# Attention and routed experts on one Trainium2 core: one load per head for both row tiles of a pair, and smaller pieces of the first experts' weights

## The chip, the cores and the metric

The kernel runs on one core of a Trainium2 chip. The metric is the device time of one execution in microseconds (us), lower is better. Engines are called TensorE (PE, with its weight loads as PEld), VectorE (DVE), ScalarE (ACT), GpSimd (POOL) and SyncE (SP), which only issues transfers here.

## What is computed

Two parts follow one another. First, local attention over chunks of 64 positions; then a mixture of eight experts in which each token goes to one expert and each expert keeps at most `capacity` tokens (80).

```python
q_c, k_c, v_c = (a.reshape(B, H, nc, 64, D) for a in (q, k, v))   # B=8, H=8, S=576, D=64
scores = q_c @ k_c.transpose(0, 1, 2, 4, 3) / 8
attn = exp(scores - scores.max(-1)); attn /= attn.sum(-1) + 1e-9
x = (attn @ v_c) as (B*S, H*D) = (4608, 512)

logits = x @ w_gate                       # 8 experts
e = argmax(logits); gate = softmax(logits)[e]
for e in range(8):                        # at most 80 tokens each, those of the largest gate
    out[tok] = gate[tok] * (relu(x[tok] @ w1[e]) @ w2[e])   # 512x1024 and 1024x512, f32
```

Rows of `out` whose token was not kept are zero.

## The kernel before

**Attention.** The 4608 rows are 36 row tiles of 128, taken as 18 pairs (`NPAIR`). A tile's queries and keys are 128 rows of 1024 f32 in memory (`qk`). They go into a tile of three parts of 512 columns (`qb`), the rows of one head half at columns 0 to 1023 and those of the other at 512 to 1535, each on every second partition; the corners stay zero from memsets at the start, so that one matmul does two heads. Each tile therefore has two loads of 64 rows of 4 KB (`load_qk`, L320 to L325), 256 KB each. The values have two loads of 64 rows of 2080 bytes per tile (`load_v`, L330 to L332), 130 KB each. Six buffers of each kind hold three pairs.

The loop over pairs (L688 to L734) is software-pipelined. Step n runs the scores of pair n (L341, 32 matmuls), the transposes of finished rows of pair n-3 (`px`, L366), the values of pair n-2 (L394), the transposes of probabilities of pair n-1 (`pt`, L366), on VectorE the maxima and differences of pair n and the division of pair n-2, and then the store of pair n-2 to scratch (`xs`, L422, 512 KB). Every second step has the gate's matmuls for four tiles (L446) and the steps of the gating chain. The transfers of a step are all issued by SP, in the order in which the program writes them: after `scores(n)` the first tile of pair n+3, then the values of the first tile of pair n+1, the second tile of pair n+3, the values of the second tile, then the store. An instruction that waits on SP holds up everything behind it. `order` below is that program order.

**Opening** (L635 to L672). VectorE and GpSimd clear the buffers; TensorE runs 25 matmuls on a cleared tile (`warm`); SP issues queries and keys of pairs 0, 1 and 2, values of pairs 0 and 1, the constants (`ct`, `wgp`, `capi`), and the values of pair 2. Pair 3 is issued in step 0, after all of these.

**Weights of the first two experts.** `EARLY` names the steps at which pieces of experts 0 and 1 are issued (`early_weights`, L622 to L633): eight pieces of 1 MB, pieces 0 to 5 at steps 15 to 19 (18 and 19 stand for the two places behind the loop), pieces 6 and 7 behind it. The last two are held back by a small copy on GpSimd into the target (L630) that reads a column of `bo`, a result of the gating chain.

**Selection** (L736 to L888). The end of the gating chain finds each expert's threshold, ranks the tokens kept and makes the lists of rows. `hot` (L585) makes the one-hot matrices: five of them by VectorE into tiles `pk` that take over the memory of five `qb` buffers. `keep_warm` (L607) runs matmuls whose result nobody reads. GpSimd then gathers the kept rows from `xs`, six indirect transfers of 128 rows (`gather`, L175); the first one ends TensorE's wait.

**Experts** (L171 to L278). Six row tiles go through both layers (`hc` L202, `yc` L235). The third expert's first weights are issued by `part(2, 0)` (L916) ahead of the gathers; the rest, and the stores of zeros to `out`, follow by the list `LATER`, each `part` of list 0 only after a gathered tile has landed (L905). Of the names in the listings, `w1_2` is the first layer's weights of expert 2.

Of the kernel before, what the change touches and what calls it, by code (L numbers as in the profile page):

```python
# [21 lines left out]
NB = 3  # L22
NBV = 6
NT = 9
# [16 lines left out]

EARLY = {15: [0], 16: [1], 17: [2, 3], 18: [4], 19: [5]}

# [12 lines left out]
def attention_moe(ctx: ExitStack, tc: tile.TileContext, qk, vv, wg, w1, w2, cap, cst, out):  # L56
# [225 lines left out]
    with ExitStack() as actx:  # L282
# [14 lines left out]
        TT = {}  # L297
        QKV = {}
        XT = {}
# [13 lines left out]
        def flush(queue):  # L313
            while queue:
                step_one(queue)

        qbufs = [wk.tile([P, 3 * 512], F32, name=f"qb{j}", tag=f"qb{j}", bufs=1)
                 for j in range(2 * NB)]

        def load_qk(i, eng=nc.sync):  # L320

            d = QKV["qk", i] = qbufs[i % (2 * NB)]
            for h in range(2):
                eng.dma_start(d[h:P:2, 512 * h:512 * h + 1024],  # L324
                              qk[i // 2, i % 2, 64 * h:64 * h + 64])  # L325

        vbufs = [wk.tile([P, 2, VW], F32, name=f"vb{j}", tag=f"vb{j}", bufs=1)
                 for j in range(NBV)]

        def load_v(i):  # L330
            for h in range(2):
                nc.sync.dma_start(vbufs[i % NBV][h:P:2, h], vv[i // 2, i % 2, h])  # L332

        def scores(n):
            d = U[n] = {}
            ps = d['s'] = ps1.tile([P, 2, 512], F32, name=f"s{n}", tag="o" if n == 1 else "s")
            for t in range(2):
                t8 = QKV["qk", 2 * n + t].rearrange("p (w a u s) -> p w a u s", w=3, a=4, u=2)
                for pr in range(4):
                    for u in range(2):  # L340
                        nc.tensor.matmul(  # L341
                            ps[64 * u:64 * u + 64, t, P * pr:P * pr + P].rearrange(
                                "p (h k) -> p h k", h=2),
                            lhsT=t8[:, 1, pr, u, :], rhs=t8[:, 0:3:2, pr, u, :],
                            start=True, stop=True)
# [31 lines left out]
        def values(i, tag=None):  # L377
# [3 lines left out]
            if r == 0:  # L381
                TT[T] = wk.tile([P, 4, DM], F32, name=f"x{T}", tag="x")
            v = vbufs[i % NBV].rearrange("p h (a u x) -> p h a u x", a=4, u=2)
            if tag is None:
# [200 lines left out]
        def hot(rt, way, n):  # L585

            if way == "v":
                j = S['hot'] = S.get('hot', -1) + 1
                oh = wk.tile([P, P, HOT], BF16, name=f"pk{rt}", tag=f"qb{j}", bufs=1)
                nc.vector.tensor_tensor(  # L590
# [31 lines left out]
        def early_weights(n, after=None):  # L622

            e, c = divmod(n, 4)
            if c == 0:
                weights[e] = tiles_w(wp, e)
            j = c % 2
            w, src, m = ((weights[e][0], w1, 2), (weights[e][1], w2, 4))[c // 2]
            if after is not None:
# [5 lines left out]
        with tc.manual_schedule():  # L635
            warm = gk.tile([P, 2 * P], BF16, name="warm", tag="lv", bufs=LV)
            nc.vector.memset(warm, 0.0)
            for j, qb in enumerate(qbufs):
                eng = nc.gpsimd if j == 1 else nc.vector
                eng.memset(qb[:, 0:512], 0.0)  # L640
                eng.memset(qb[:, 1024:1536], 0.0)  # L641
                if j < 2:
                    load_qk(j, (nc.sync, nc.scalar)[j])
            nc.scalar.dma_start(ident, cst[:, C_ID:C_ID + P])
            for j, vb in enumerate(vbufs):
                (nc.vector if j in (0, 2) else nc.gpsimd).memset(vb, 0.0)
            nc.vector.memset(wgp[:, :, 8:32], 0.0)
# [11 lines left out]
            nc.scalar.mul(idp, ident, float(P))  # L659
            for i in (2, 3):  # L660
                load_qk(i)
            for i in (0, 1):
                load_v(i)
            for i in (4, 5):
                load_qk(i)
            for i in (2, 3):
                load_v(i)
            nc.sync.dma_start(ct[:, C_ID + P:], cst[:, C_ID + P:])
            nc.sync.dma_start(wgp[:, :, 0:8], wg.rearrange("(b p) e -> p b e", p=P))
            nc.sync.dma_start(capi, cap[0:1, :].broadcast_to([P, 2]))  # L670
            for i in range(4, NBV):
                load_v(i)  # L672

# [14 lines left out]
            for n in range(NPAIR):  # L688
                odd = n % 2
                if n == 2:  # L690
                    late_constants()
                scores(n)
                if n + NB < NPAIR:
                    load_qk(2 * (n + NB))
                    if n < 2:
                        load_qk(2 * (n + NB) + 1)
                if n >= 5 and odd:
# [3 lines left out]
                if n >= 2:  # L701
                    for t in range(2):
                        values(2 * (n - 2) + t)
                        if n - 2 + NBV // 2 < NPAIR:
                            load_v(2 * (n - 2) + t + NBV)
                        if t == 0 and n + NB < NPAIR:
                            load_qk(2 * (n + NB) + 1)
                if n >= 1:
# [71 lines left out]
            for j in range(33, 36):  # L780
                steps_(nc.vector, j)
            for k in (6, 7):
                early_weights(k, bo[:, 28 + 4 * (k - 6):29 + 4 * (k - 6)])
            tally(28, 4)
# [88 lines left out]

            keep_warm(6)

# [194 lines left out]
```

## Time and profile before

| | us |
|---|---|
| three timed runs | 259.73, 262.20, 262.93 (median 262.20) |
| the profiled execution | 259.46 |
| its span, first to last instruction | 257.7 |

The span is what the profile shows; the remaining 1.8 us of the profiled execution lie outside it. All times in the rows are us from the start of the span. A row with "x" and a number merges that many instructions; what stands in brackets or behind "<-" is what ended the idle time before it. The granted clock (PEclk) is TensorE's clock as a share of 2.4 GHz; 0.5 is 1.2 GHz.

### The profile page before, as it was taken

The page shows a single profiled execution, that of the slowest core. Times are in us where ns is not written, and L with a number is a line of the kernel's source. Part 1 is how long each engine was busy: PE and PEld are TensorE (multiplying, and loading weights), DVE is VectorE, ACT ScalarE, POOL GpSimd, SP SyncE. Part 2 cuts the span into 40 slices and gives each one's busy share as a digit, 9 for nine tenths or more (in the row PEclk, how much of TensorE's full clock was granted, in tenths as well). Part 3 has the DMA queues.
Part 4 walks back from the last instruction along what each step waited for, and adds up shares of the span by engine and source line. Part 5 has one row for each costly group of instructions (what it writes and reads, how often), then busy time and mean ns, then how long its engine had stood idle before and what let it go on. Part 6 is the DMA issues. An engine that isn't in the chain of part 4 may idle for free.

```text
span 257.7 us, 7341 instructions
## 1 busy us (share of the span) xinstructions
PE 227.0 (88%) x3117; PEld 145.5 (56%) x3117; DVE 118.7 (46%) x263; ACT 66.2 (26%) x115; POOL 56.9 (22%) x167
## 2 busy tenths in 40 slices
PE   6851999999999988798878858999999999999990
PEld 4751988898889877687756742343433434333320
DVE  7924376967869675677658360111111102112200
ACT  1202133535537352536354001120100202001000
POOL 9003000023332222213848354000000000000261
PEclk9998599999999999999997795999999999999996
DMA  5868999999999989999999998999999999999240
GB/s 206 282 217 243 365 346 327 308 326 320 304 311 334 315 293 317 310 318 295 332 405 413 410 392 281 401 393 411 416 409 401 416 408 413 410 397 404 111 156 36
DMA packets 35766, 84.73 MB, mean 329 GB/s; under 512 B 4048, under 2 KB 4176, under 8 KB 35728
## 3 DMA queue, kind: packets, MB, share of 16 engines
q1 hardware_dynamic: 34464, 80.73, 86.8%
q0 software_dynamic: 960, 2.88, 3.1%
q10 hardware_dynamic: 304, 0.59, 0.7%
q8 instruction: 27, 0.44, 0.7%
q14 instruction: 11, 0.09, 0.1%
HBM read 64.00 MB, written 20.45 MB: 328 GB/s over the span
## 4 chain that ended last, share of the span: by engine, by line
PE 68%; DMA 10%; SPq 9%; DVE 4%; POOL 3%; issue 3%; ACT 0%; POOLq 0%; DVEq 0%
PE hc L202 17%; PE yc L235 16%; PE o L394 10%; PE s L341 9%; DMA qb<-in_qk 5%; SPq L332 5%; PE px L366 4%; SPq L324 3%; PE small L446 3%; PE pt L366 3%; DMA vb<-in_vv 3%; DMA xgc<-xs,gic 2%; PE hpc L220 2%; PE xpc L190 1%; DVE qb L641 1%
## 5 line engine op out<-in xcount | busy, mean ns | idle before, releaser
L341 PE MATMUL s<-qb 128*64 128x128 f32 x576 | 38.1, 284 | 13.1 <-DMA qb<-in_qk 12.9
L202 PE MATMUL hc<-w,xtc 128*32 128x512 f32 x384 | 45.5, 619 | 0.0
L235 PE MATMUL yc<-w,htc 128*32 128x512 f32 x384 | 42.3, 592 | 0.0
L341 PEld LDWEIGHTS s<-qb 128*64 128x64 f32 x576 | 32.7, 141 | 16.8 <-issue 10.7
L394 PE MATMUL o<-vb,pT 128*64 128x130 f32 x576 | 36.4, 278 | 1.0 <-DMA vb<-in_vv 1.0
L351 DVE TENSOR_REDUCE mx<-s 128x16 f32<-128x1024 f32 x18 | 22.0, 1224 | 25.7 <-PE s L341 25.7
L394 PEld LDWEIGHTS o<-vb,pT 128*64 128x64 f32 x576 | 31.9, 136 | 2.2 <-PE px L366 1.1
L235 PEld LDWEIGHTS yc<-w,htc 128*32 128x32 f32 x384 | 12.4, 110 | 28.3 <-issue 28.3
L202 PEld LDWEIGHTS hc<-w,xtc 128*32 128x32 f32 x384 | 12.1, 114 | 27.8 <-issue 27.4
L375 ACT ACTIVATE pT<-pt 128x1024 f32<-128x1024 f32 x18 | 18.4, 1024 | 28.9 <-PE pt L366 28.9
L437 ACT COPY xT<-px 128x1024 f32<-128x1024 f32 x17 | 17.2, 1011 | 33.5 <-PE px L366 33.5
L254 POOL DMA_INDIRECT out<-ysc,to x6 | 6.0, 994 | 88.4 <-SPq L921 84.7
L409 DVE TENSOR_TENSOR x<-o,rc 128x1024 f32<-128x1024 f32 (+1 forms) x20 | 22.4, 1118 | 0.7
L356 DVE TENSOR_TENSOR sm<-s,mx 128x1024 f32<-128x1024 f32 x18 | 22.1, 1229 | 0.6
L207 ACT ACTIVATE hsc<-hc 128x512 f32<-128x512 f32 x6 | 3.6, 598 | 65.3 <-PE hc L202 65.3
L240 DVE TENSOR_SCALAR ysc<-yc,gatec 128x512 f32<-128x512 f32 x6 | 4.5, 752 | 33.4 <-PE yc L235 33.4
L209 DVE TENSOR_SCALAR hsc<-hc 128x512 f32<-128x512 f32 x6 | 4.2, 692 | 26.6 <-PE hc L202 26.6
L224 DVE COPY htc<-hpc 128x512 f32<-128x512 f32 x6 | 4.2, 692 | 22.0 <-PE hpc L220 22.0
L366 PE MATMUL pt<-ct,sm 64*128 64x64 f32 x288 | 12.8, 229 | 1.6 <-ACT pT L375 1.2
L366 PE MATMUL px<-ct,x 64*128 64x64 f32 x288 | 13.2, 234 | 0.0
L511 POOL TENSOR_SCALAR u<-sx 128x4 f32<-128x4 f32 x8 | 1.6, 195 | 52.4 <-DVE sx L510 40.8
L366 PEld LDWEIGHTS pt<-ct,sm 64*128 64x128 f32 x288 | 10.4, 139 | 4.8 <-issue 2.8
(133 smaller groups left out, 226.3 us busy)
## 6 DMA issues: line engine op xcount, KB each, us to landing
w<-in_w SPq DMA_DIRECT2D x12, 2048.0 KB, 17.6
qb<-in_qk SPq DMA_DIRECT2D x70, 256.0 KB, 4.8
vb<-in_vv SPq DMA_DIRECT2D x72, 130.0 KB, 4.3
out<-zero SPq DMA_DIRECT2D x9, 1024.0 KB, 16.9
xs<-x SPq DMA_DIRECT2D x16, 512.0 KB, 4.6
w<-in_w SPq DMA_DIRECT2D x8, 1024.0 KB, 11.7
xs<-x SPq DMA_DIRECT2D x4, 256.0 KB, 10.5
qb<-in_qk ACTq DMA_DIRECT2D x2, 256.0 KB, 3.6
```

The lines of the kernel that those rows point to most:

```text
L202: nc.tensor.matmul(h[o:o + 32, :], lhsT=xT[r][:, b, o:o + 32], rhs=getw(groups[r][g])[0][:, b, 512 * f:512 * f + 512], start=(b == 0), sto ...
L235: nc.tensor.matmul(y[o:o + 32, :], lhsT=hT[r][c // 4][:, c % 4, o:o + 32], rhs=getw(groups[r][g])[1][:, c, :], start=(c == 0), stop=(c == ...
L324: eng.dma_start(d[h:P:2, 512 * h:512 * h + 1024], qk[i // 2, i % 2, 64 * h:64 * h + 64])
L332: nc.sync.dma_start(vbufs[i % NBV][h:P:2, h], vv[i // 2, i % 2, h])
L341: nc.tensor.matmul(ps[64 * u:64 * u + 64, t, P * pr:P * pr + P].rearrange("p (h k) -> p h k", h=2), lhsT=t8[:, 1, pr, u, :], rhs=t8[:, 0:3 ...
L351: nc.vector.tensor_reduce(d['mx'], d['s8'], axis=AX.X, op=ALU.max)
L356: nc.vector.tensor_tensor(d['sm'].rearrange("p c k h -> p h c k"), d['s8'], d['mx'][:, :, :, None].to_broadcast([P, 2, 8, 64]), op=ALU.sub ...
L366: nc.tensor.transpose(pm[:, u, 64 * c:64 * c + 64], src(c)[rows], ident[rows, rows])
L375: nc.scalar.activation(d['pT'], pt, AF.Exp, scale=0.125)
L394: nc.tensor.matmul(po[64 * u:64 * u + 64, o:o + 130].rearrange("p (h x) -> p h x", h=2), lhsT=d['pT'][:, u, c:c + 64], rhs=v[:, :, pr, u, ...
L409: nc.vector.tensor_tensor(TT[T][:, r:r + nt, :].rearrange("p r (k h e) -> p (r k) h e", k=4, h=2), pov[..., 0:64], rc[:, :, :, None].to_br ...
L437: nc.scalar.copy(dst, pm)
```

## The change

- `load_qk(n)` and `load_v(n)` load one head half of both row tiles of a pair with one transfer: 64 rows, two pieces of 4 KB each (512 KB), and two pieces of 2080 bytes (260 KB). A pair has 5 transfers instead of 9. The buffers are three tiles of double size. `load_qk(n + 3)` is issued after all of the scores of pair n, `load_v(n + 1)` after both tiles' values of pair n-2.
- In the opening the two loads of pair 0 are issued by SP and ScalarE, pair 1 and 2 by SP; the constants and the values of pair 2 move behind the queries and keys of pair 3. The memsets of `qb` are all on VectorE, that of `warm` on GpSimd. `late_constants` runs in step 4 instead of 2.
- The weights of experts 0 and 1 go in 16 pieces of 512 KB. By the end of the loop's last place (19) ten pieces (5 MB) are issued instead of 6 MB; the other six wait for copies on GpSimd, two behind `bo` column 28 and four behind column 32.
- The five `pk` matrices lie in one buffer (`qb2`). `keep_warm(6)` before the gather is `keep_warm(10)`.
- `part(2, 0)` stands where it stood, ahead of the gathers, in both programs; what changes is what it waits for (below).

```diff
-EARLY = {15: [0], 16: [1], 17: [2, 3], 18: [4], 19: [5]}
+EARLY = {15: [0], 16: [1, 2], 17: [3, 4], 18: [5, 6, 7], 19: [8, 9], 20: [10, 11], 21: [12, 13, 14, 15]}
...
-        def load_qk(i, eng=nc.sync):
-            d = QKV["qk", i] = qbufs[i % (2 * NB)]
+        qbufs = [wk.tile([P, 2, 3 * 512], F32, name=f"qb{j}", tag=f"qb{j}", bufs=1)
+                 for j in range(NB)]
+        def load_qk(n, engs=(nc.sync, nc.sync)):
             for h in range(2):
-                eng.dma_start(d[h:P:2, 512 * h:512 * h + 1024],
-                              qk[i // 2, i % 2, 64 * h:64 * h + 64])
+                engs[h].dma_start(qbufs[n % NB][h:P:2, :, 512 * h:512 * h + 1024],
+                                  qk[n, :, 64 * h:64 * h + 64].rearrange("t p f -> p t f"))
...
-        def load_v(i):
+        def load_v(n):
             for h in range(2):
-                nc.sync.dma_start(vbufs[i % NBV][h:P:2, h], vv[i // 2, i % 2, h])
+                nc.sync.dma_start(vbufs[n % NB][h:P:2, :, h],
+                                  vv[n, :, h].rearrange("t p f -> p t f"))
...
-                j = S['hot'] = S.get('hot', -1) + 1
-                oh = wk.tile([P, P, HOT], BF16, name=f"pk{rt}", tag=f"qb{j}", bufs=1)
+                if 'hot' not in S:
+                    S['hot'] = wk.tile([P, 5, P, HOT], BF16, name="pk", tag="qb2", bufs=1), deque(range(5))
+                oh = S['hot'][0][:, S['hot'][1].popleft()]
...
-            e, c = divmod(n, 4)
+            e, c = divmod(n, 8)
...
-            nc.vector.memset(warm, 0.0)
+            nc.gpsimd.memset(warm, 0.0)
             for j, qb in enumerate(qbufs):
-                eng = nc.gpsimd if j == 1 else nc.vector
-                eng.memset(qb[:, 0:512], 0.0)
-                eng.memset(qb[:, 1024:1536], 0.0)
-                if j < 2:
-                    load_qk(j, (nc.sync, nc.scalar)[j])
+                nc.vector.memset(qb[:, :, 0:512], 0.0)
+                nc.vector.memset(qb[:, :, 1024:1536], 0.0)
+                if j == 0:
+                    load_qk(0, (nc.sync, nc.scalar))
...
+            load_qk(1)
+            load_qk(2)
+            load_v(0)
+            load_v(1)
...
                 scores(n)
                 if n + NB < NPAIR:
-                    load_qk(2 * (n + NB))
-                    if n < 2:
-                        load_qk(2 * (n + NB) + 1)
+                    load_qk(n + NB)
+                    if n == 0:
+                        nc.sync.dma_start(ct[:, C_ID + P:], cst[:, C_ID + P:])
+                        nc.sync.dma_start(wgp[:, :, 0:8], wg.rearrange("(b p) e -> p b e", p=P))
+                        nc.sync.dma_start(capi, cap[0:1, :].broadcast_to([P, 2]))
+                        load_v(2)
...
                         values(2 * (n - 2) + t)
-                        if n - 2 + NBV // 2 < NPAIR:
-                            load_v(2 * (n - 2) + t + NBV)
-                        if t == 0 and n + NB < NPAIR:
-                            load_qk(2 * (n + NB) + 1)
+                    if n - 2 + NB < NPAIR:
+                        load_v(n - 2 + NB)
...
-            for k in (6, 7):
-                early_weights(k, bo[:, 28 + 4 * (k - 6):29 + 4 * (k - 6)])
+            for k in EARLY[20]:
+                early_weights(k, bo[:, 28:29])
+            for k in EARLY[21]:
+                early_weights(k, bo[:, 32:33])
...
-            keep_warm(6)
+            keep_warm(10)
```

The first place is SP in one step of the attention loop. Before, with what each instruction waits for (`DMAHW0` to `DMAHW7` are eight counters of landed loads, taken in turn; `PE_49` and `DVE_49` are those engines' counters):

```order
L324 DMA qb_99<-in_qk 64x1024 [waits DMAHW5_49,PE_49]
L324 DMA qb_99<-in_qk 64x1024 [waits DMAHW6_49]
L332 DMA vb_107<-in_vv 64x520 [waits DMAHW7_49,PE_49]
L332 DMA vb_107<-in_vv 64x520 [waits DMAHW0_49]
L324 DMA qb_100<-in_qk 64x1024 [waits DMAHW1_49]
L324 DMA qb_100<-in_qk 64x1024 [waits DMAHW2_49]
L332 DMA vb_108<-in_vv 64x520 [waits DMAHW3_49,PE_49]
L332 DMA vb_108<-in_vv 64x520 [waits DMAHW4_49]
L422 DMA xs<-x_299 128x2x512 [waits DMAHW5_49,DVE_49]
```

and the same step now:

```order
L320 DMA qb_99<-in_qk 64x2x1024 [waits DMAHW1_49,PE_49]
L320 DMA qb_99<-in_qk 64x2x1024 [waits DMAHW2_49]
L328 DMA vb_103<-in_vv 64x2x520 [waits DMAHW3_49,PE_49]
L328 DMA vb_103<-in_vv 64x2x520 [waits DMAHW4_49]
L419 DMA xs<-x_258 128x2x512 [waits DMAHW5_49,DVE_49]
```

Nine transfers of a step became five, in the same order of kinds; each load carries twice the rows' bytes.

The second place is SP between the weights of expert 1 and those of expert 3, that is, up to and behind the gathers. Before:

```order
L631 DMA w2_1_2225<-in_w2 128x4x512 [waits DMAHW6_49,Pool_49]
L631 DMA w2_1_2225<-in_w2 128x4x512 [waits DMAHW7_49,Pool_49]
L906 DMA w1_2_2711<-in_w1 128x4x1024 [waits DMAHW0_49,DVE_49,PE_49]
L906 DMA w2_2_2737<-in_w2 128x8x512 [waits DMAHW1_49,DVE_49]
L906 DMA w1_3_2740<-in_w1 128x4x1024 [waits DMAHW2_49,DVE_49]
```

and now:

```order
L629 DMA w2_1_2198<-in_w2 128x2x512 [waits DMAHW6_49,Pool_49]
L629 DMA w2_1_2198<-in_w2 128x2x512 [waits DMAHW7_49,Pool_49]
L897 DMA w1_2_2636<-in_w1 128x4x1024 [waits DMAHW0_49]
L897 DMA w2_2_2662<-in_w2 128x8x512 [waits DMAHW1_49,DVE_49,PE_49]
L897 DMA w1_3_2665<-in_w1 128x4x1024 [waits DMAHW2_49,DVE_49,PE_49]
```

The load of `w1_2` waited for VectorE and TensorE (the `pk` matrices and the matmuls that read them lay in its memory) and no longer does; it can go as soon as the pieces ahead of it have gone.

The third place is GpSimd in the selection, where the held-back pieces' copies stand between the last part of one gating block and the next. Before:

```order
L499 CAST comp_76<-r24_2029 128x4x8 [waits Pool_49]
L630 COPY w2_1_2225<-bo_78 128x1
L630 COPY w2_1_2225<-bo_78 128x1 [waits DVE_49]
L519 TENSOR_TENSOR kb_79<-mine_77,bb28_2295 128x4x8
L522 TENSOR_SCALAR gg28_2292<-sx28_2291 128x4
```

and now:

```order
L496 CAST comp_76<-r24_1943 128x4x8 [waits Pool_49]
L628 COPY w1_1_2197<-bo_78 128x1 x2
L628 COPY w2_1_2198<-bo_78 128x1 [waits DVE_49]
L628 COPY w2_1_2198<-bo_78 128x1 x3
L516 TENSOR_TENSOR kb_79<-mine_77,bb28_2212 128x4x8
L519 TENSOR_SCALAR gg28_2209<-sx28_2208 128x4
```

Two copies became six; three more stand behind the one that waits.

## Rows read from the trace of the kernel before

**Rows 1.** Chain that ended last, in order of time: start, length, what.
```profile
21.47 4.17 DMA qb<-in_qk
25.77 3.73 PE s L341 x32
33.50 1.90 PE s L341 x32
...
86.42 1.05 PE s L341 x16
...
148.93 6.41 DMA xgc<-xs,gic
155.47 1.09 PE xpc L190 x4
156.59 5.80 PE hc L202 x32
...
212.55 3.43 PE hc L202 x32
```

**Rows 2.** Waits of TensorE: us in total, times, longest.
```profile
PE s L341 <- DMA qb<-in_qk: 12.9, 8, 5.4
...
PE o L394 <- DMA vb<-in_vv: 1.0, 1, 1.0
```

**Rows 3.** Timeline of SP, one step of the loop: start, us, line, count.
```profile
38.81 1.43 SPq L324 DMA_DIRECT2D qb<-in_qk  x2
40.34 1.17 SPq L332 DMA_DIRECT2D vb<-in_vv  x2
41.55 1.52 SPq L324 DMA_DIRECT2D qb<-in_qk  x2
43.17 1.42 SPq L332 DMA_DIRECT2D vb<-in_vv  x2
44.69 0.75 SPq L422 DMA_DIRECT2D xs<-x  x1
```

**Rows 4.** Stretches: busy PE, PEld, DVE, ACT, POOL; granted clock, DMA share, GB/s.
```profile
24.00:32.00 8.00, 6.23 (x68) 5.66 (x70) 2.43 (x2) 1.02 (x1) 0.00 (x0) 0.57 0.95 341
32.00:86.00 54.00, 54.00 (x1076) 48.08 (x1076) 42.17 (x76) 25.10 (x39) 9.48 (x42) 1.00 0.95 321
...
128.00:149.00 21.00, 17.54 (x210) 13.61 (x203) 12.62 (x52) 6.94 (x19) 11.52 (x38) 0.84 1.04 410
...
154.00:161.00 7.00, 5.49 (x28) 1.82 (x32) 0.46 (x3) 0.75 (x2) 3.20 (x4) 0.51 0.88 283
```

**Rows 5.** DMA packets from 27 to 34 us.
```profile
DMA packets 1023, 2.66 MB, mean 381 GB/s; under 512 B 182, under 2 KB 182, under 8 KB 1022
```

**Rows 6.** DMA issues of the page: count, size, median us to landing.
```profile
qb<-in_qk ACTq DMA_DIRECT2D x2, 256.0 KB, 3.6
```

**Rows 7.** Timeline of the opening: VectorE's first memset of a buffer.
```profile
1.04 0.48 DVE L640 MEMSET qb<- 128x512 f32 x1
```

**Rows 8.** Timeline: TensorE, the scores of the last pair.
```profile
113.99 1.97 PE L341 MATMUL s<-qb 128*64 128x128 f32 x32
```

**Rows 9.** Timeline of the selection: GpSimd, SP and TensorE.
```profile
135.38 0.19 POOL L630 COPY w<-bo 128x1 f32<-128x1 f32 x1 [0.86 <-DVE bo L517]
...
135.92 0.52 POOL L522 TENSOR_SCALAR gg<-sx 128x4 f32<-128x4 f32 x2
...
143.69 0.37 SPq L906 DMA_DIRECT2D w<-in_w  x1
...
151.09 0.83 PE L612 MATMUL pwarm<-io_b,ones_b 128*128 128x256 bf16 x6
```

**Rows 10.** DMA issues from 143 to 144 us: size, us to landing.
```profile
w<-in_w SPq DMA_DIRECT2D x1, 2048.0 KB, 12.0
```

**Rows 11.** DMA issues from 152 to 155 us: median us to landing.
```profile
xgc<-xs,gic POOLq DMA_INDIRECT x3, 4.1
```

**Rows 12.** DMA issues from 194 to 197 us: first weights of expert 6.
```profile
w<-in_w SPq DMA_DIRECT2D x1, 2048.0 KB, 16.8
```

More of the change, by code (lines that the diff above doesn't have):

```diff
@@ L22 @@
 NB = 3
-NBV = 6
 NT = 9
@@ L297, in attention_moe @@
         TT = {}
-        QKV = {}
         XT = {}
@@ L315, in flush @@
                 step_one(queue)
-        qbufs = [wk.tile([P, 3 * 512], F32, name=f"qb{j}", tag=f"qb{j}", bufs=1)
-                 for j in range(2 * NB)]
-        def load_qk(i, eng=nc.sync):
-            d = QKV["qk", i] = qbufs[i % (2 * NB)]
+        qbufs = [wk.tile([P, 2, 3 * 512], F32, name=f"qb{j}", tag=f"qb{j}", bufs=1)
+                 for j in range(NB)]
+        def load_qk(n, engs=(nc.sync, nc.sync)):
             for h in range(2):
-                eng.dma_start(d[h:P:2, 512 * h:512 * h + 1024],
-                              qk[i // 2, i % 2, 64 * h:64 * h + 64])
-        vbufs = [wk.tile([P, 2, VW], F32, name=f"vb{j}", tag=f"vb{j}", bufs=1)
-                 for j in range(NBV)]
-        def load_v(i):
+                engs[h].dma_start(qbufs[n % NB][h:P:2, :, 512 * h:512 * h + 1024],
+                                  qk[n, :, 64 * h:64 * h + 64].rearrange("t p f -> p t f"))
+        vbufs = [wk.tile([P, 2, 2, VW], F32, name=f"vb{j}", tag=f"vb{j}", bufs=1)
+                 for j in range(NB)]
+        def load_v(n):
             for h in range(2):
-                nc.sync.dma_start(vbufs[i % NBV][h:P:2, h], vv[i // 2, i % 2, h])
+                nc.sync.dma_start(vbufs[n % NB][h:P:2, :, h],
+                                  vv[n, :, h].rearrange("t p f -> p t f"))
         def scores(n):
@@ L337, in scores @@
             for t in range(2):
-                t8 = QKV["qk", 2 * n + t].rearrange("p (w a u s) -> p w a u s", w=3, a=4, u=2)
+                t8 = qbufs[n % NB][:, t].rearrange("p (w a u s) -> p w a u s", w=3, a=4, u=2)
                 for pr in range(4):
@@ L382, in values @@
                 TT[T] = wk.tile([P, 4, DM], F32, name=f"x{T}", tag="x")
-            v = vbufs[i % NBV].rearrange("p h (a u x) -> p h a u x", a=4, u=2)
+            v = vbufs[n % NB][:, t].rearrange("p h (a u x) -> p h a u x", a=4, u=2)
             if tag is None:
@@ L622, in early_weights @@
         def early_weights(n, after=None):
-            e, c = divmod(n, 4)
+            e, c = divmod(n, 8)
             if c == 0:
                 weights[e] = tiles_w(wp, e)
-            j = c % 2
-            w, src, m = ((weights[e][0], w1, 2), (weights[e][1], w2, 4))[c // 2]
+            l, j = divmod(c, 4)
+            w, src, m = ((weights[e][0], w1, 1), (weights[e][1], w2, 2))[l]
             if after is not None:
@@ L636, in attention_moe @@
             warm = gk.tile([P, 2 * P], BF16, name="warm", tag="lv", bufs=LV)
-            nc.vector.memset(warm, 0.0)
+            nc.gpsimd.memset(warm, 0.0)
             for j, qb in enumerate(qbufs):
-                eng = nc.gpsimd if j == 1 else nc.vector
-                eng.memset(qb[:, 0:512], 0.0)
-                eng.memset(qb[:, 1024:1536], 0.0)
-                if j < 2:
-                    load_qk(j, (nc.sync, nc.scalar)[j])
+                nc.vector.memset(qb[:, :, 0:512], 0.0)
+                nc.vector.memset(qb[:, :, 1024:1536], 0.0)
+                if j == 0:
+                    load_qk(0, (nc.sync, nc.scalar))
             nc.scalar.dma_start(ident, cst[:, C_ID:C_ID + P])
             for j, vb in enumerate(vbufs):
-                (nc.vector if j in (0, 2) else nc.gpsimd).memset(vb, 0.0)
+                (nc.vector, nc.gpsimd, nc.gpsimd)[j].memset(vb, 0.0)
             nc.vector.memset(wgp[:, :, 8:32], 0.0)
@@ L659, in attention_moe @@
             nc.scalar.mul(idp, ident, float(P))
[L660 to L672, printed above, removed]
+            load_qk(1)
+            load_qk(2)
+            load_v(0)
+            load_v(1)
             def late_constants():
@@ L689, in attention_moe @@
                 odd = n % 2
-                if n == 2:
+                if n == 4:
                     late_constants()
```

## Prediction

> **What bounds the kernel now.** I read the chain that ended last first, then TensorE's waits, then SP's timeline, then the rates by stretch. The chain [rows 1] is TensorE nearly throughout, with three gaps. The reader is to see the first at 21.47 us: the scores of pair 3 start only at 25.77 us, when their load has landed, and take 3.73 us, twice the 1.90 us of pair 4 at 33.50 us. From there to the first scores of pair 13 at 86.42 us the chain has no wait: nine steps in 52.92 us, 5.88 us each. Then waits for `qb` come back: the scores of pair 17 start at 113.99 us [rows 8], four steps in 27.57 us, 6.89 us each. TensorE waited 12.9 us for `qb` in all, and 1.0 us for the last values [rows 2]. The last gap is the first gather, 6.41 us.
>
> Why loads that were in time at 40 us are late at 90 us is seen on SP [rows 3]. One step is nine transfers, and issuing them takes 1.43 + 1.17 + 1.52 + 1.42 + 0.75 = 6.29 us; with the small gaps it runs from 38.81 to 45.44 us, 6.6 us. TensorE needs 5.88 us. So SP loses some 0.7 us a step, the lead of three pairs is used up after some ten steps, and then SP sets the pace. The transfers move 321 GB/s there [rows 4]: a step is 4 x 262 KB + 4 x 133 KB + 524 KB = 2.105 MB.
>
> **The steps of the change and their price.** All against the profiled execution: 259.46 us.
>
> A, the opening. To start pair 3, four pairs of queries and keys (4.19 MB), two of values (1.06 MB) and the identity (0.07 MB) must have come: 5.32 MB. The first load waits for a memset of twice the width, 2 x 0.48 us from 1.04 us at the latest [rows 7], so it goes at 2.0 us. A load of 256 KB landed after 3.6 us there [rows 6], of which 0.7 us is its own transfer; 2.9 us stay as latency. SP issues the eleven transfers of its own up to there in about 11 x 0.6 us behind memsets that end by some 9 us, so it is not in the way; the transfer rate is. Its nearest rows are 341 GB/s from 24 to 32 us [rows 4], 381 GB/s in the busiest seven us of mixed loads and stores [rows 5] and 321 GB/s where SP limits. I take 341: 2.0 + 2.9 + 15.6 = 20.5 us for pair 3. Pair 4 needs 1.92 MB more (its own, values of pair 2, constants), 5.6 us: 26.1 us instead of 33.50. **-7.4 us** (at 321 GB/s 21.5 and 27.5 us, so -6.0; at 381 23.9 us, so -9.6). Part of it is the clock: it was granted at 0.57 from 24 to 32 us, mostly the 1.2 GHz level, after TensorE had waited for the load; with no such wait the level stays 2.4 GHz.
>
> B, the steps. SP issues five transfers, about 5 x 0.6 = 3.0 us (no row has one of 512 KB of this kind; the 512 KB store took 0.75 us, so at most 3.8 us). SP is no longer late; next is TensorE with 5.88 us, if 2.105 MB come in that time: 358 GB/s. Rows 5 say yes (381), the 341 of rows 4 no (6.17 us). I take TensorE's pace, since the 381 holds for the same mix with a full queue, and a wait for the landing of the eighth transfer before now covers twice the bytes. Pairs 4 to 13 keep their 52.92 us; 13 to 17 take 4 x 5.88 = 23.5 instead of 27.57: **-4.1 us**. The merged load waits for both tiles' scores, and stands ahead of values and store on SP; it is needed three steps later, so that costs nothing as long as landing stays under some 12 us.
>
> C, the last values. Only 512 KB of weights instead of 1 MB stand ahead of them, and SP issues them in time: **-1.0 us**, TensorE's wait.
>
> D, the held-back copies. Four more on GpSimd, three of them behind the copy at 135.38 us, from where GpSimd is on the chain to the ranking. One costs 0.19 us alone and 0.26 us by the pair at 135.92 [rows 9]: **+0.7 us** (0 to 1.0).
>
> E, the gather. Before, the 2 MB of `w1_2` were issued at 143.69 us [rows 9], after `pk`, and landed 12.0 us later [rows 10], at 155.7 us; the first gather, issued at 148.93, landed beside it after 6.41 us. Now `w1_2` does not wait for `pk`. The gather is issued at 148.93 - 7.4 - 4.1 - 1.0 + 0.7 = 137.1 us. Behind the loop (from about 110 us) two stores, eleven pieces and `w1_2` remain, 8.9 MB, at 410 GB/s [rows 4] 22 us: done by some 132 us. So the gather meets an idle queue. Three later gathers took 4.1 us [rows 11]: **-2.3 us** (0 if the queue is still full).
>
> F, the clock after it. TensorE's last matmuls before the gather end at 151.92 us [rows 9], it then stands until 155.47, and the granted clock from 154 to 161 us is 0.51, the 1.2 GHz level [rows 4]: the first 32 `hc` matmuls take 5.80 us, later ones 3.43 [rows 1]. Four more warm matmuls (0.14 us each) and a gather 2.3 us shorter leave some 0.7 us of standing, and the clock should not fall: 2.4 us. But the weights follow: the first ones of expert 6, issued at about 194.05 us, landed 16.8 us later [rows 12], at 210.8, for matmuls at 212.55 [rows 1]. Only those 1.7 us are free. **-1.7 us** (0 if the clock falls).
>
> Sum: -7.4 - 4.1 - 1.0 + 0.7 - 2.3 - 1.7 = -15.8, that is 243.7 us beside 259.46. The profiled execution is 0.3 us below the fastest timed run and 2.7 us below the median of 262.2, so a median is likelier somewhat above such a sum; I add 1 us: **244.7 us**.
>
> A rule against the change: the Trainium skill, "DMA: Bandwidth & Descriptors", Issuing engines are not separate DMA queues, says that the sequencer's time to initiate a transfer "is usually small relative to the DMA itself". By it, fewer issues would give nothing and B and most of A would be zero. Rows 3 disagree for these sizes: an issue takes about 0.6 us, and 133 KB move in 0.35 us at 381 GB/s.
>
> **Rivals.**
>
> R1, the transfers bind already. For it: their engines' share is 0.95 at 321 GB/s [rows 4]. Then a step stays 6.56 us: pair 3 at 21.5, pair 17 at 21.5 + 14 x 6.56 = 113.3 instead of 113.99. With C nil and D to F as above: 259.46 - 0.7 + 0.7 - 4.0 + 1 = 256.5 us, and 260.5 if the gather finds a full queue. Against it: 381 GB/s in rows 5, where SP had just issued a row of loads back to back.
>
> R2, between: 341 GB/s, 6.17 us a step, 13 steps cost 3.8 us more: 248.5 us; 252.5 without E and F.
>
> R3, slower: the new form of load goes over few of the 16 transfer engines. The source's two row tiles stand far apart, and if a transfer were split by the two tiles instead of the 64 rows, two engines would carry it: 410 / 16 = 26 GB/s each, 1.58 MB of loads a step at 51 GB/s are 31 us, 18 steps 558 us, some 690 us in all. It decides from 14 engines down (358 / 410 x 16). Against it: the order shows 64 rows outermost at the target, and `w1_1` was loaded before in the same three-level form, 128x2x1024, in the stretch with 410 GB/s. The Trainium skill has the rule in "DMA: Bandwidth & Descriptors", Why a DMA increments its semaphore by 16 and not by 1: as many engines, up to 16, as divide the outermost sizes of both sides; by that it depends on which side's order the instruction carries, and 64 gives 16.
>
> R4, all goes well: A at 381 GB/s and F whole, 259.46 - 9.6 - 4.1 - 1.0 + 0.4 - 2.3 - 2.4 + 1 = 241.5 us; a gather still quicker takes it to 239.
>
> **Chances and range.** The forecast (242 to 247) 0.50, R2 0.22, R4 0.13, R1 0.12, R3 0.03. The range of 238 to 255 holds the first three of these, less a little at each end, and leaves out R3 and most of R1: about 0.8. About 2% either way is what a measurement of this kernel can tell from no change: 257 and 267.4 us. Faster: all but R3 and most of R1, 0.86; within 2%: 0.10; slower: 0.04.
>
> **What would show it.** Right: pair 3's scores at 19 to 21 us at full clock, no wait for `qb` from then on, SP idle a third of each step, pair 17's scores near 102.5 us, 350 GB/s or more from 32 to 86 us, the first gather within some 4 us of its issue near 137 us, the first 32 `hc` matmuls in about 3.5 us. Wrong: waits of TensorE for `qb` at every step with the rate still near 320 GB/s (R1), a step of 6.1 to 6.3 us (R2), loads that land after tens of us (R3), a first gather of 6 us or more (E), or GpSimd's chain longer by over 1 us (D).

## The result, and the profile after

The changed kernel took 247.07 us (median of four runs, 246.04 to 248.35) beside 260.97 us for the kernel before: a ratio of 0.949, 95% interval 0.940 to 0.959. Its profiled execution took 246.04 us with a span of 244.2 us. The forecast was 244.7 us, its range 238 to 255 us. Ratios, here and below, leave out runs that were over 1.5% above the fastest of their kernel.

The chain that ended last in the changed kernel (start, length, what), to be read beside [rows 1] and [rows 8]:

```profile
12.85 6.55 DMA qb<-in_qk
19.54 1.97 PE s L338 x32
...
25.97 1.97 PE s L338 x32
...
32.16 1.90 PE s L338 x32
...
102.51 1.90 PE s L338 x32
...
112.77 1.93 PE o L391 x32
...
122.66 0.70 POOL w L628 x4
...
136.92 4.68 DMA xgc<-xs,gic
...
142.61 3.64 PE hc L201 x32
...
196.73 17.13 DMA w<-in_w
...
213.90 3.63 PE hc L201 x30
```

The reader sees pairs 3, 4 and 5 at 19.54, 25.97 and 32.16 us, pair 17 at 102.51, no wait for a load between them, the last values ending at 114.70, and two transfers that TensorE still waits for: the first gather, and behind it, new, the first weights of the last expert. TensorE's waits (us in total, times, longest), beside [rows 2]:

```profile
PE s L338 <- DMA qb<-in_qk: 3.2, 3, 1.4
PE xpc L189 <- DMA xgc<-xs,gic: 1.4, 1, 1.4
...
PE hc L201 <- DMA w<-in_w: 0.2, 1, 0.2
```

The wait for `qb` is 3.2 us instead of 12.9, all of it in the opening. One step on SP, beside [rows 3], is five transfers that take 1.25 + 1.26 + 0.36 = 2.87 us to issue, not 6.29:

```profile
34.17 1.25 SPq L320 DMA_DIRECT2D qb<-in_qk  x2
36.92 1.26 SPq L328 DMA_DIRECT2D vb<-in_vv  x2
38.68 0.36 SPq L419 DMA_DIRECT2D xs<-x  x1
```

The stretches, beside [rows 4] (busy PE, PEld, DVE, ACT, POOL; granted clock, share of the transfer engines, GB/s):

```profile
20.00:32.00 12.00, 10.75 (x220) 9.63 (x216) 7.93 (x10) 4.29 (x6) 2.39 (x7) 1.00 1.02 398
32.00:86.00 54.00, 54.00 (x1061) 48.10 (x1053) 41.85 (x80) 25.40 (x42) 11.22 (x50) 1.00 1.03 390
86.00:114.00 28.00, 26.82 (x536) 23.66 (x532) 21.94 (x49) 14.94 (x26) 9.97 (x41) 1.00 0.85 291
115.00:136.00 21.00, 16.90 (x215) 13.15 (x204) 12.40 (x49) 6.92 (x19) 13.52 (x42) 0.84 1.01 364
```

The same loads move at 390 GB/s instead of 321 with TensorE busy throughout; from 86 to 114 us there is little left to load (291 GB/s, share 0.85), and behind that the weights fill the queue. The issues of `w1_2` and of the first gather (size, us to landing), beside [rows 10]:

```profile
w<-in_w SPq DMA_DIRECT2D x1, 2048.0 KB, 14.2
...
xgc<-xs,gic POOLq DMA_INDIRECT x1, 4.7
```

`w1_2` was issued at 126.96 us and so landed at 141.1, after the gather's issue at 136.92.

Against the terms of the sum, in us:

| term | predicted | measured | from |
|---|---|---|---|
| A, pair 4 | -7.4 | -7.5 | 33.50 to 25.97 |
| B, pair 17, less A | -4.1 | -4.0 | 113.99 to 102.51 |
| C, end of the last values, less A and B | -1.0 | -1.1 | 127.28 to 114.70 |
| D, last values to the gather's issue | +0.7 | +0.6 | 21.65 to 22.22 |
| E, gather, issue to landing | -2.3 | -1.7 | 6.41 to 4.68 |
| F, first gathered transpose to the end | -1.7 | +0.2 | 102.2 (155.47 to 257.7) to 102.5 (141.74 to 244.2) |
| sum | -15.8 | -13.5 | span 257.7 to 244.2 |

So in this execution the forecast's miss is E and F. What the other terms rest on was not shown by this agreement, and was tried. A second execution of the same kernel, further down, splits D and E otherwise: there D is -1.0 and E +0.1.

### The profile page after: what moved, and what is told of

Its sections match the earlier page's. It is cut to its first block, busy times and chain, and to the rows that moved or that the text cites. A ratio compares the mean times of both kernels' runs of the same rounds, so it can differ in the third digit from the quotient of the medians.

```text
span 244.2 us, 7221 instructions
## 1 busy us (share of the span) xinstructions
PE 224.2 (92%) x3121; PEld 143.5 (59%) x3121; DVE 119.1 (49%) x257; ACT 65.8 (27%) x115; POOL 56.6 (23%) x168
## 4 chain that ended last, share of the span: by engine, by line
PE 70%; DMA 14%; SPq 5%; DVE 3%; POOL 3%; issue 2%; ACT 1%; POOLq 0%; DVEq 0%; ACTq 0%
PE o L391 13%; PE hc L201 13%; PE s L338 13%; PE yc L234 11%; DMA w<-in_w 7%; PE px L363 5%; DMA qb<-in_qk 5%; SPq L616 4%; PE pt L363 4%; PE small L443 4%; PE hpc L219 2%; DMA xgc<-xs,gic 2%; PE small L453 1%; PE pwarm L610 1%; PE xpc L189 1%
## 5 line engine op out<-in xcount | busy, mean ns | idle before, releaser
L338 PE MATMUL s<-qb 128*64 128x128 f32 x576 | 35.4, 276 | 4.4 <-DMA qb<-in_qk 3.2
L338 PEld LDWEIGHTS s<-qb 128*64 128x64 f32 x576 | 31.2, 137 | 7.2 <-DVE x L406 2.4
L434 ACT COPY xT<-px 128x1024 f32<-128x1024 f32 x17 | 17.1, 1008 | 25.3 <-PE px L363 25.3
L533 ACT ACTIVATE lv<-io_b,bo 128x256 bf16<-128x256 bf16 x29 | 12.5, 498 | 0.4 <-DVE bo L514 0.4
```

Of the source, the lines that this page charges most:

```text
L338: nc.tensor.matmul(ps[64 * u:64 * u + 64, t, P * pr:P * pr + P].rearrange("p (h k) -> p h k", h=2), lhsT=t8[:, 1, pr, u, :], rhs=t8[:, 0:3 ...
L434: nc.scalar.copy(dst, pm)
L533: nc.scalar.activation(lv, io_b, AF.Sign, bias=bo[:, rt:rt + 1], scale=-1.0)
```

## The experiments

Eleven more runs were made, one of them of the changed kernel itself. Ratios are against runs of the kernel before on the same chip.

**All loads split again.** The order of the changed kernel, but one load for each row tile:

```diff
-            for h in range(2):
-                engs[h].dma_start(qbufs[n % NB][h:P:2, :, ...], qk[n, :, ...])
+            for t in range(2):
+                for h in range(2):
+                    engs[h].dma_start(qbufs[n % NB][h:P:2, t, ...], qk[n, t, ...])
```

and the same in `load_v`.

> The changed kernel with every merged load split again by row tile (nine transfers a step on SP, same order of kinds, buffers and waits). Theory S (the number of issues on SP sets the pace): SP needs 6.3 to 6.7 us a step again, the rate from 32 to 86 us falls from 390 to 310-340 GB/s, TensorE waits for qb again in the last third of the loop, pair 17's scores come at 106 to 109 us instead of 102.5, the kernel takes 250 to 253 us. Rival T (larger transfers use the transfer engines better, SP was never the limit): the same slow rate here, so this run alone does not tell them apart; e2 does. Rival O (only the opening's order gave the gain): steps stay at 5.9 us, no waits for qb after pair 4, pair 17 at 103 us, 247 us.

Measured: 259.82 us, ratio 1.000 (0.996 to 1.003). The whole gain is gone, more than was expected (250 to 253 us). Its chain, pairs 5 and 17, and one step on SP:

```profile
35.03 1.90 PE s L339 x32
...
112.87 1.90 PE s L339 x32
```

```profile
59.35 2.88 SPq L321 DMA_DIRECT2D qb<-in_qk  x4
62.33 2.47 SPq L330 DMA_DIRECT2D vb<-in_vv  x4
64.89 0.54 SPq L420 DMA_DIRECT2D xs<-x  x1
```

Twelve steps take 77.84 us, 6.49 each; in the changed kernel the same twelve take 70.35 (32.16 to 102.51), 5.86 each. SP is issuing for 5.89 of 6.17 us in the step shown. But pair 4 started at 27.4 us, its second tile at 29.71, well ahead of the kernel before (33.50). The stores, which SP issues last in each step, show why this early start comes to nothing: the first and the thirteenth in the kernel before,

```profile
31.12 0.53 SPq L422 DMA_DIRECT2D xs<-x  x1
...
112.01 0.53 SPq L422 DMA_DIRECT2D xs<-x  x1
```

and here:

```profile
30.84 0.53 SPq L420 DMA_DIRECT2D xs<-x  x1
...
111.40 0.81 SPq L420 DMA_DIRECT2D xs<-x  x1
```

SP's own step is 6.74 us before and 6.71 us here: the same. TensorE's steps are shorter than SP's, 6.19 us before (33.50 to 113.99, 13 steps) and 6.49 here, because it uses up its lead over SP; here it starts earlier and the lead is gone sooner. Pair 17 comes at nearly the same time, 112.87 beside 113.99.

**Only the opening's loads split** (`n < 5`; the others merged):

> The changed kernel with the loads of pairs 0 to 4 split by row tile again (their order is that of the change) and those of pairs 5 to 17 merged. In the kernel with all loads split, pair 4 had its scores at 27.4 us (changed kernel 26.0, kernel before 33.4) and the 13 pairs behind it took 6.57 us each (changed kernel 5.88). If the order is what brings the opening forward, as that says, and the merged loads what keeps the steps short: pair 4 at 26.5 to 28, pair 5 at 32 to 35, pair 17 at 102.5 to 106, and 247 to 250 us in all. If my prediction's first term (fewer issues in the opening, 7.4 us) is due to the merged loads, and the early pair 4 there was chance: pair 4 at 30 to 33.5, pair 17 at 107 to 110, 251 to 255 us.

Measured: 249.13 us, ratio 0.961 (0.954 to 0.968); pair 4 at 28.7 us, its second tile at 29.9, and on the chain pairs 5 and 17:

```profile
35.24 1.90 PE s L349 x32
...
105.59 1.90 PE s L349 x32
```

70.35 us for the twelve steps, the changed kernel's to the last digit. So the opening's gain has two sources: with the new opening alone (its order, memsets and first load on ScalarE) pair 5 comes at 35.24 us instead of 39.62, with merged loads too at 32.16. The steps' gain comes from the merged loads, and without it the opening's is lost by pair 17, as the run before shows.

**The loads by themselves.** Why does a step with nine loads take over 6 us? Two kernels had no arithmetic, only the transfers.

> This kernel leaves out all the arithmetic: it only moves the loads of ten pairs and a 512 KB store beside each, four times over, with no wait on another engine's work: first the split loads of the kernel before, all nine transfers of a pair issued by SyncE; second the merged ones, five transfers; third the split ones issued in turn by SyncE and ScalarE, the store by SyncE; fourth the merged ones with four more loads of 512 bytes between them, nine issues again, all by SyncE. It separates three readings of the shorter step (6.20 us a pair before, 5.88 after, 6.57 when only the loads are split again). Theory S, SyncE's time for issues: 6.2 to 6.7 us a pair in the first part with SyncE waiting for no landing, 5.0 to 5.6 in the second, 5.0 to 5.6 in the third, since each engine issues half, and 6.0 to 6.7 in the fourth. Theory T, the transfers themselves (many small ones move at 314 to 321 GB/s, fewer large ones at 390, whoever issues them): 6.2 to 6.7 in the first and in the third, 5.0 to 5.6 in the second and, since four times 512 bytes are next to nothing, in the fourth. Theory W, a wait of every issue for the landing of the eighth transfer before it: SyncE is seen waiting for landings in the first and the fourth part.

In the first part a pair took 6.18 us (nine pairs in 55.58 us), 341 GB/s, and SP waited for no landing. The fourth part took 6.54 us a pair, but with SP waiting for landings 12 times, 10.3 us in 58: that the tiny loads take places among the eight counters (theory W) fits this, SP's time alone does not. But a tiny load is 128 packets of 4 bytes: packets under 512 bytes rose from 1286 in the first part's stretch to 5347 in this one, so the transfers themselves (theory T) may be what is slower. The parts between ran into each other, since ScalarE, waiting for nothing of SP's, went ahead. So once more, in another order:

> As the kernel that only moves loads (no arithmetic, ten pairs a part), where the part with ScalarE ran beside the merged part and told nothing by itself. Now three parts one behind the other: the split loads issued in turn by SyncE and ScalarE; the merged loads by SyncE; the split loads by SyncE. In the first such run the last of these took 6.18 us a pair with SyncE issuing without a pause and waiting for no landing. Theory S, SyncE's time for issues: first part 5.0 to 5.6 us a pair, second 5.0 to 5.6, third 6.1 to 6.3. Theory T, small transfers move more slowly whoever issues them: first part 6.0 to 6.5. Theory W, an issue waits for the landing of the eighth transfer before it, counted over both engines: the first part in between, with SyncE or ScalarE seen waiting for a landing most of the time; the merged part waits as well, but with twice the bytes in flight.

The three parts in their steady stretches (no engine computes; busy DVE, POOL; clock, share of the transfer engines, GB/s):

```profile
4.00:52.00 48.00, 0.00 (x0) 0.00 (x0) 1.00 1.00 352
68.00:109.00 41.00, 0.00 (x0) 0.00 (x0) 1.00 1.04 413
118.00:147.00 29.00, 0.00 (x0) 0.00 (x0) 1.00 0.99 347
```

With 2.105 MB a pair that is 5.98 us for split loads from two engines, 5.10 for merged loads, 6.07 for split loads from SP. In the last part SP never stops:

```profile
123.39 0.59 SPq L70 DMA_DIRECT2D xs<-x  x1
124.02 2.78 SPq L76 DMA_DIRECT2D qb<-in_qk  x4
126.84 2.51 SPq L80 DMA_DIRECT2D vb<-in_vv  x4
129.40 0.58 SPq L70 DMA_DIRECT2D xs<-x  x1
```

while in the merged part it waits for landings at four issues of five, 17.6 us of 41 (the longest row of SP's waits from 68 to 109 us):

```profile
SPq L70 <- DMA qb<-in_qk: 5.3, 8, 0.7
...
```

Nine loads from one engine are bound by issuing, since SP never pauses; five are bound by the transfers. SP's step of 6.74 us in the kernel before is longer than these 6.07 to 6.18: it also waited 7.4 us from 32 to 86 us, by the profile mostly for TensorE; what the waits were was not tried. Theory S holds for one engine; it failed for two, where 5.0 to 5.6 was expected. What binds there is open between two theories. As theory W has it, SP waited for landings 29.8 us of those 48. But the transfer engines' share was 1.00, and the loads of queries and keys, in the first part and in the last, took longer to land at nearly the same rate:

```profile
qb<-in_qk ACTq DMA_DIRECT2D x18, 256.0 KB, 5.2
```

```profile
qb<-in_qk SPq DMA_DIRECT2D x20, 256.0 KB, 4.6
```

That more loads in flight only wait longer fits theory T, small transfers that are slower whoever issues them, whose lower bound of 6.0 was missed by 0.02.

**The second tiles' queries and keys issued by ScalarE**, from pair 3 on, with split loads:

```diff
+                    (nc.scalar if t and n > 2 else engs[h]).dma_start(
```

> As e1 with nine transfers of the old size a step, but the two qk loads of the second row tile are issued by ScalarE's queue (from pair 3 on), so SP issues seven, some 4.3 us a step. Theory S: the pace is TensorE's again, 5.9 us a step, no waits for qb after pair 4, pair 17 at 102.5 to 105 us, 370 GB/s or more from 32 to 86 us, 246 to 249 us. Rival T (transfer size decides): as slow as e1, 310-340 GB/s, pair 17 at 106 to 109 us, 250 to 253 us.

Measured: 261.81 us, ratio 1.005 (1.000 to 1.010): nothing gained, against theory S's 246 to 249 (theory T's "as slow as e1" came out, not its 250 to 253). SP's own step was shorter, 6.32 us (stores from 35.82 to 111.70), but the opening was late: pair 4 at 33.11 us. The longest of SP's waits for landings, and a copy of ScalarE (what ended its idle time in brackets):

```profile
SPq L331 <- DMA qb<-in_qk: 7.6, 5, 4.1
```

```profile
43.84 1.01 ACT L436 COPY xT<-px 128x1024 f32<-128x1024 f32 x1 [4.21 <-DMA qb<-in_qk]
```

The eight counters are dealt out in program order over both engines. The 4.1 us are of this kind: the values' load at 34.61 us waited for the counter of a load that ScalarE had issued at 29.46, behind its own work, and that landed at 34.55. And a load of ScalarE that waits for a counter holds up the copy behind it: ScalarE was idle for 4.21 us here, some 1.7 of them after the copy's input was done (`px`, at 42.11 us). Two engines in one ring of counters wait for each other.

**The third expert's first weights behind the gather** (`(2, 0)` first in `LATER`, waiting for the first gathered tile):

> The first weights of expert 2 are issued behind the first gather's landing instead of ahead of the gather. Theory Q (the gather's 4.7 us are shared with those 2 MB, which landed beside it in both kernels): the first gather lands 2.7 to 3.6 us after its issue; then the chain of weights is 5.2 us longer from there, TensorE waits for weights for 4 to 6 us more in the expert stage, 250 to 252 us. Rival (the gather's time is its own): still 4.5 us or more from issue to landing.

Measured: 251.34 us, ratio 0.972 (0.964 to 0.980). The gather takes 3.7 us now, and TensorE waits for weights:

```profile
PE hc L201 <- DMA w<-in_w: 2.6, 1, 2.6
```

So the gather's 4.7 us were the queue ahead of it. But every later weight follows this load: 1 us is won at the gather, and the whole takes about 4 us more than the changed kernel.

**The pieces of the first two experts earlier**, into the stretch from 86 to 114 us:

```diff
-EARLY = {15: [0], 16: [1, 2], 17: [3, 4], 18: [5, 6, 7], 19: [8, 9], 20: [10, 11], 21: [12, 13, 14, 15]}
+EARLY = {14: [0], 15: [1, 2, 3], 16: [4, 5, 6], 17: [7, 8, 9], 18: [10, 11], 19: [12], 20: [13], 21: [14, 15]}
```

> The changed kernel with the 512 KB pieces of the first two experts issued earlier, into the time from 86 to 114 us in which the transfers run at 291 GB/s: one behind pair 14, three each behind pairs 15, 16 and 17, where none, one, two and two stood, so that four instead of eight wait for the end of attention. If the first gather's 4.7 us is a queue that still empties (the third expert's first weights landed at 141.1 us, behind the gather's issue at 136.9): those weights land at 134 to 138 and the gather takes 3.3 to 3.8 us from issue to landing, 1 us gained at the gather; the whole time then 245 to 247, since the expert stage behind it still waits for the weights of expert 7, which hang on the same gather. Rival: the pieces delay the last loads of attention or the stores, pair 17's scores come later than 103.5 and the gather is issued after 138: 247.5 to 250.

Measured: 244.74 us, ratio 0.943 (0.936 to 0.949). `w1_2`, issued at 124.60 us, landed after 11.3 us, at 135.9, and the gather, issued at 135.77, after 3.6:

```profile
w<-in_w SPq DMA_DIRECT2D x1, 2048.0 KB, 11.3
...
xgc<-xs,gic POOLq DMA_INDIRECT x1, 3.6
```

as expected; the whole is 0.3 us below the expected 245 to 247. TensorE's wait for weights grew to 1.0 us.

**The last weights ahead of zeros.** Three stores of zeros behind the last expert's first weights:

```diff
-[(4, 1), (5, 1), (2, 2)], [(6, 0), (6, 1), (3, 2), (4, 2), (7, 0)]
+[(4, 1), (5, 1)], [(6, 0), (6, 1), (7, 0), (2, 2), (3, 2), (4, 2)]
```

> Three stores of zeros move behind the first weights of experts 6 and 7 in the list of the expert stage. Theory W (the stage ends with the chain of transfers behind the gather; TensorE's clock gain was lost in waits of 0.2 and over 1 us for the first weights of experts 6 and 7, and in the matmuls just ahead of them): both land 2.5 to 7 us earlier, no wait of TensorE for weights is left, the time from the gather's landing to the end falls by 2.0 to 2.4 us, 244.5 to 245.5 us. Rival Z (the zeros' landing before the scatter ends the kernel): TensorE is earlier by as much, but the scatter waits, 246.5 to 248 us.

Measured: 246.50 us, ratio 0.947 (0.941 to 0.953). No wait for weights is left, but the time is above the 244.5 to 245.5 of this run's theory W. The chain ends in TensorE's work and, behind it, in GpSimd's writes of the results, the last of which starts 0.8 us after VectorE has its rows ready (238.94 beside 238.10): the start of what rival Z expected. From the first gathered transpose (143.24 us) to the end are 101.7 us. The granted clock from 140 to 147 us was 0.76, and the first 32 `hc` matmuls took 4.52 us.

**The changed kernel once more.**

> The changed kernel once more, word for word, beside the run without holds on the same chip: 245.5 to 248.5 us, and 2.5 to 4 us above that run if the gains of the early pieces and of the order are real and not a difference of chips.

Measured: 246.79 us, ratio 0.947 (0.943 to 0.952). This execution differs from the first by chance in D, E and F. Its chain:

```profile
134.91 6.55 DMA xgc<-xs,gic
...
141.59 1.08 PE xpc L189 x4
...
142.71 5.51 PE hc L201 x32
```

The gather was issued 2.0 us earlier than in the first profile and landed at the same time, 141.46 beside 141.60: the queue sets the landing. So D, from the last values (114.28 us) to the issue, is 20.63 us here and not 22.22, and E is 6.55 us and not 4.68; their sum moved by 0.3 us only. TensorE stood 3.2 us for it, the granted clock from 140 to 147 us was 0.53, and the first 32 `hc` matmuls took 5.51 us instead of 3.64. Now no weights were waited for, and from the first transpose to the end were again 102.3 us. What the clock takes, the weights' waits give back.

**Both: earlier pieces and the new order of weights.**

> The changed kernel with the pieces of the run before and, as in the run with the weights ahead of the zeros, three stores of zeros moved behind the last expert's first weights. That run showed no wait for weights any more and 101.7 us from the first gathered transpose to the end, 0.8 less than the changed kernel although its first 32 matmuls ran 0.9 us longer at a low granted clock. If both waits are what is left over: the gather as in the run before, no wait for weights in the expert stage, 100.7 to 101.7 us from the first transpose to the end, 243 to 245.5 us. Rival: the granted clock falls behind the gather and takes it back: 245.5 to 247.5.

Measured: 244.02 us, ratio 0.940 (0.934 to 0.946). The gather took 3.5 us; TensorE's waits from 134 us on:

```profile
PE xpc L189 <- DVE nf L873: 0.6, 1, 0.6
PE hc L201 <- ACT xtc L191: 0.2, 1, 0.2
```

With neither a fall of the clock in it nor a wait of TensorE for weights the stretch from the first transpose (139.47 us) to the end is 101.5 us. It is little shorter than the 101.7 us of the run with the weights first, and something else now ends the kernel: GpSimd's six writes of the results to `out`:

```profile
228.16 1.04 POOL L253 DMA_INDIRECT out<-ysc,to  x1 [83.57 <-SPq L912]
...
235.51 0.98 POOL L253 DMA_INDIRECT out<-ysc,to  x1 [0.28 <-POOL to L252]
```

The first starts about when the last zeros land (issued at 213.6 us, 14.4 us to landing), the others follow one behind the other, and the last starts 2.3 us after VectorE has its rows ready (233.20 us). In the changed kernel it was 0.8 us (238.62 beside 237.84).

**No piece held back** (all sixteen by step 19, on top of the last kernel):

> The kernel with early pieces and the changed order, and now all sixteen pieces are issued by the end of the last store's step and none is held by a copy on POOL. My prediction put the four copies more that the change brought to POOL's path at 0.7 us (0.19 each), and the trace of the changed kernel has four of them as one piece of 0.70 us on the chain. If they are on the path that sets the gather: the selection, from the last values to the gather's issue, is 0.4 to 0.7 us shorter than in the run before (two copies were left there), and the whole 0.3 to 0.8 us less, 243.2 to 243.8 beside 244.0. If the last sums on DVE, which the copies wait for, are the path anyway: the same time within 0.3 us. Rival: three more pieces ahead of the third expert's first weights delay the stores or the gather by their 1.3 us each: 244.5 to 246.

Measured: 243.30 us (243.01 to 245.86), ratio 0.936 (0.932 to 0.941): the fastest version, 3.5 us below the changed kernel in the same set of runs. The gain over the run before lies within the intervals. In the profile the way from pair 17's scores to the gather's issue is shorter by some 0.3 us, less than the 0.4 to 0.7 expected, though two copies are gone. The writes of the results again run one behind the other to the end (227.78 to 235.12 us). In the selection GpSimd waits instead:

```profile
124.04 0.24 POOL L483 TENSOR_TENSOR keys<-mine,gg 128x32 f32<-128x32 bf16 x1 [1.00 <-DVE gg L521]
```

## Why the prediction was right, and where it was not

A was right in its number and in its reason: the sum counted the bytes ahead of pairs 3 and 4 at a transfer rate and said that SP is not in the way. The run with only the opening split bears out the order, which alone brings pair 4 from 33.50 to 28.7 us (second tile 29.9); the rest needs the merged loads. Inside the term two errors cancel, by luck: pair 3 came 1.0 us earlier, at 19.54 us instead of 20.5, at 362 GB/s from 4 to 20 us, not the 341 taken; pair 4 came 6.4 us behind it instead of 5.6, and no longer for its load alone, which landed at 25.83 us, but as much for VectorE's division, which on the chain ends at 25.86.

B was right in its number: SP set the pace of the kernel before, and TensorE that of the changed one. Its reason is shown for one engine: nine issues take 6.07 to 6.18 us with nothing else to do, five leave SP pauses. The term counts only four steps because a lead hides SP's 6.74 us in the other nine, and an earlier opening alone uses that lead up sooner. So with split loads A and B are lost together, and the merged loads are worth more than 4.1 us in the new order; the old order with merged loads was not tried. R1 and R2 fall: the transfers can carry a pair in 5.10 us if the loads are large. With small loads R1 is not far off, 5.98 us a pair from two engines at a share of 1.00. That a wait "for the landing of the eighth transfer before now covers twice the bytes" is what the merged part shows: SP waits at four issues of five and the queue still moves 413 GB/s.

C came out, and was not tried by itself.

D's number came out in the first execution by luck: in the second execution of the same kernel D is -1.0 us (21.65 to 20.63), and the spread between the two, 1.6 us, is larger than the term. As a price of copies it is not shown either: without any of them GpSimd waits 1.00 us for VectorE's `gg` at the same place. The prediction named what is behind the copies, not what would be late without them.

E was right in its direction in the first execution and 0.6 us too large; in the second the gather took 6.55 us, no less than before. The step that failed is "done by some 132 us. So the gather meets an idle queue". The pieces behind the copies were issued from 121.98 us on, `w1_2` only at 126.96, and the rate from 115 to 136 us was 364 GB/s, not 410 (280 from 118 to 122 us, when the pieces were still held back). So `w1_2` landed at 141.1 us, behind the gather's issue. Emptied in time, as by the earlier pieces, the queue gives 3.5 to 3.7 us.

F failed. Its premise held in the first profiled execution (the clock stayed at the 2.4 GHz level, first `hc` 3.64 us instead of 5.80) and not in the second (5.51), but "only those 1.7 us are free" was read at expert 6 alone. At expert 7 the weights, issued at 196.73 us, landed 17.1 us later, at 213.86. The first 32 matmuls that need the weights of expert 6, from 196.22 us on, took 4.87 us, and those of expert 7 4.74 us, against 3.62 without a wait:

```profile
197.46 3.63 PE L201 MATMUL hc<-w,xtc 128*32 128x512 f32 x28 [0.21 <-DMA w<-in_w]
...
212.80 4.74 PE L201 MATMUL hc<-w,xtc 128*32 128x512 f32 x32
```

That is 2.4 us lost, of which the 0.2 us in the rows of TensorE's waits are the smallest part (its weight loads waited 2.1 us more). The faster clock had given 1.9 (5.51 to 3.64). The chain of transfers behind the gather is as long as TensorE's work, so a faster TensorE waits: with either clock the stretch takes 102.3 to 102.5 us. With the weights ahead of the zeros it shrinks to 101.5 to 101.7 us, and then GpSimd's writes behind the zeros hold the end.

R3 did not happen, at 390 GB/s. Of the Trainium skill's sentence weighed there ("DMA: Bandwidth & Descriptors", Issuing engines are not separate DMA queues), the premise does not hold here: nine issues take 6.1 us, the same bytes in five loads 5.1. Its conclusion, that issuing from a second engine gains little, does (6.07 to 5.98 us a pair); whether for the waits for landings or for the transfers' own pace is open.

## What to carry to other kernels

Where the loads of a step come from one queue, add up what issuing them takes and compare it with the step of the bottleneck engine. Measure it on the issuing engine, since a lead can hide its pace from the bottleneck's steps (6.74 and 6.19 us here). Halving the number of loads by a larger access pattern did more here than a second issuing engine (5.10 against 5.98 us a pair), which shared the counters of loads in flight and stalled the work behind its issues. When a transfer must be quick (a gather), look for a stretch with an unfilled queue ahead of it and move bulk loads there, and do not delay the loads that a later chain hangs on. Before booking a gain of the compute engine, look at the slack of every later load, not of the next one, and at what waits for the last transfer.

## What the runs showed of the hardware that was not expected

- An issue by SP takes about 0.6 us back to back, whether the load carries 130 or 512 KB: 2.51 us for four value loads, 1.25 us for two merged ones of queries and keys. Behind a wait the store takes 0.36 us, back to back 0.59.
- Four loads of 512 bytes among the merged loads of a pair cost as much as splitting these: 6.54 us a pair at 321 GB/s beside 5.10 at 413. Each of them is 128 packets of 4 bytes.
- The granted clock in the selection differs between two executions of one program: from 130 to 136 us it was 0.72 in the first profile of the changed kernel, where the transposes of the ranking (`kr`) ran, and the gather was issued 34.4 us behind pair 17's scores (102.51 to 136.92); it was 1.00 in the second, with 32.8 us (102.09 to 134.91). That is 1.6 us of spread without any change.
